# Two buffers for the split second weight of the small slots, and its split and gather moved

## The chip, the cores and the metric

The kernel runs on one core of one Trainium2 chip. It is written by hand for the five engines: PE (TensorE, matmuls), DVE (VectorE), ACT (ScalarE), POOL (GpSimd, which also issues the indirect DMAs: gathers and scatters by a list of rows) and SP (SyncE, which issues plain DMAs). The metric is the device time of one execution in microseconds (us).

## The reference

An attention over channels is followed by a mixture of experts in which each token takes one expert, or none. In short:

```python
qn = q / (norm(q, axis=1) + 1e-06); kn = k / (norm(k, axis=1) + 1e-06)
s = kn.transpose(0, 2, 1) @ qn / tau            # B = 4, N = 5056, C = 256
a = softmax(s)                                  # 256 x 256 for each of the 4
x = (v @ a).reshape(20224, 256)

do_compute = x @ w_skip > 0                     # the other tokens pass through
xc = x[do_compute]
e_idx = argmax(xc @ w_gate)                     # one of E = 8 experts
for e in range(8):
    h = maximum(xc[mask] @ w1[e], 0.0)          # 256 -> 1024
    y[mask] = gate_w[mask] * (h @ w2[e])        # 1024 -> 256
out[do_compute] = xc + y
```

## The kernel before

First come the scores and the attention output of the four batches, written to `out`, and the routing: each expert's tokens are written as a list of rows. The first tiles of the experts run in that stretch too. All of it is set in order by a planner from a table of costs; its tasks are emitted one after the other, and each engine executes its own instructions in the order in which they are emitted. Two loops follow. The **large loop** (L432 in the profile) takes tiles of 512 tokens of one expert, from about 467 to 746 us. The **small loop** (L522) takes what is left of each expert in slots of 128 tokens, ten of them here, two to an iteration, from 750 us to the end.

A product in this kernel is taken with operands that are split into a high part and the remainder: ACT casts the high part, DVE subtracts it from the value (`w1H`, `w1L`; `xH`, `xL`; `v2s` holds both parts of w2). The program's names in the small loop: `v1r`, `v2r` are the slot's w1 and w2 as gathered (two buffers each, 1 MB a buffer), `vc`, `vd` the indices for these gathers, copied by DVE from the table `wii`; `yg` the gathered rows, `yT` their transpose, `yr` a copy for the residual; `yH`, `yL` the split hidden layer; `yo` the slot's output; `mc`, `mN`, `mP`, `ms` the lists of rows of the present slot, of the next ones and for the scatter.

A slot has two stages. In the first, PE multiplies w1 (L539, 32 matmuls into `ph`), ACT takes the relu (L542), DVE the remainder (L543), and w2 is split in four chunks: three ahead of the first half of the hidden layer, one ahead of the second (L501 on ACT, L502 on DVE). POOL gathers w2 for the next slot, copies the list and scatters the output of the slot before (L214). In the second stage PE multiplies w2 (L558 and L559 for each of eight blocks of the hidden layer, into `po`), and after block 4 transposes the next slot's rows (L494; ACT copies `yT` and `yr`, L495 and L496). POOL gathers w1 for the slot after next and rows for it (L209). DVE ends the slot with `yo` (L564, L565).

The loops are staggered: there is no barrier between iterations, but an engine enters a stage only when every engine has signalled the end of the stage two before it. `behind(X)` puts the engine's signal at that place in its order; the instructions after it belong to the stage but aren't waited for. POOL's signal of a first stage stands behind the scatter. A loop is entered through a barrier of all engines; POOL, which collects it, may still be executing work that its sequencer has passed on.

The first rows, lists and weights of the small slots are brought in early: `load_rows` and `load_weights` are tasks of the planner and run at 457 to 468 us, ahead of the large loop (`load_weights`: w1 and w2 of slot 0, w1 of slot 1). On DVE's order the copies of the indices (L511, L512) stand there ahead of the last of the planned tiles (L344, L345) and of the splits for the first tile of the large loop (L311 for w1, L286 for x). A program's tile that is written again waits until the earlier readers are done; for a DMA that reads it, until the DMA has landed. Between the loops stands `keep_warm`, twelve small matmuls (L1129).

Of the kernel before, what the change touches and what calls it, by code (L numbers as in the profile page):

```python
# [12 lines left out]
F32R = mybir.dt.float32r  # L13
I32 = mybir.dt.int32
AF = mybir.ActivationFunctionType
ALU = mybir.AluOpType
# [4 lines left out]
P = 128  # L21
B = 4
N = 5056
C = 256
# [5 lines left out]
NFB = F // P  # L30
# [6 lines left out]
U = 2  # L37
# [106 lines left out]
def attn_moe(ctx: ExitStack, tc: tile.TileContext, q, k, vt, tau, w_skip, w_gate, w1, w2, out):  # L144
    nc = tc.nc
    V, S, G, T = nc.vector, nc.scalar, nc.gpsimd, nc.tensor
# [73 lines left out]
    def gather_w(src, to, rows):  # L220
        G.indirect_dma_start(  # L221
            out=to, out_offset=None, in_=src,
            in_offset=IndirectOffsetOnAxis(ap=rows, axis=0), bounds_check=E * P - 1, oob_is_err=False)
# [8 lines left out]
    def behind(*engines):  # L232

        for e in engines:
            tc.previous_stage_wait(e.engine)
# [3 lines left out]
    class Large:  # L239
# [191 lines left out]
        def loop(self):  # L431
            with tc.For_i(0, self.n, 1, iteration_sync="staggered", hint_engines=(mybir.EngineType.PE,)) as i, tc.manual_schedule():  # L432
                V.tensor_copy(self.wc, self.wii[:, ds(i + 1, 1)])
                V.tensor_copy(self.wd, self.wii[:, ds(i + 1, 1)])
                self.put_last()
                self.take(1)
                self.gather(1)
                gather_w(w1, self.w1r, self.wc)
                behind(G, SP)
                self.first(True)  # L440
                tc.stage_boundary()
                load_list(self.adi, i + 1, self.lN[:, :8, :], 8)
                gather_w(w2, self.w2r, self.wd)
                for t in range(4):
                    self.second(0, t)
                    if t == 1:
                        behind(T, S, V, G, SP)
                        self.transposed(1)
                tc.stage_boundary()
                self.take(0)  # L450
                self.gather(0)
                behind(G, SP)
                self.first(False)
                tc.stage_boundary()
                for t in range(4):
                    if t < 2:
                        self.split_w1(2 * t)
                        self.split_w1(2 * t + 1)
                    self.second(1, t, t < 2)
                    if t == 1:  # L460
                        self.transposed(0)
                        behind(T, S, V, G, SP)
            self.put_last()

    class Small:


        def __init__(self, adi, wii):
            self.adi, self.wii = adi, wii
            wp = ctx.enter_context(tc.tile_pool(name="ws", bufs=1, side="right", reuse_waits="tile"))  # L470
            tiles = lambda shape, dt, name: [wp.tile(shape, dt, name=f"{name}{u}") for u in range(U)]
            self.w1r = tiles([P, 2 * F], F32, "v1r")
            self.w2r = tiles([P, NFB * C], F32, "v2r")
            self.xg = tiles([P, C], F32, "yg")
            self.xr = tiles([P, C], F32, "yr")
            self.xT = tiles([P, 2, P], F32, "yT")
            self.w2s = wp.tile([P, NFB, 2, C], F32R, name="v2s")
            self.hH = wp.tile([P, NFB, P], F32R, name="yH")
            self.hL = wp.tile([P, NFB, P], F32R, name="yL")
            self.ob = tiles([P, C], F32, "yo")  # L480
            self.wc = tiles([P, 1], I32, "vc")
            self.wd = tiles([P, 1], I32, "vd")
            self.lN = tiles([P, 1, 2], I32, "mN")
            self.lP = tiles([P, 1, 2], I32, "mP")
            self.lc = tiles([P, 1, 2], I32, "mc")
            self.ls = tiles([P, 1, 2], I32, "ms")
            for u in range(U):
                V.memset(self.xg[u], 0.0)
                V.memset(self.ob[u], 0.0)
# [8 lines left out]
        def split_w2(self, u, c):  # L498
            f = slice(c * 2, c * 2 + 2)
            r = self.w2r[u][:, c * 512 : (c + 1) * 512].rearrange("p (f c) -> p f c", c=C)  # L500
            S.copy(self.w2s[:, f, 0, :], r)  # L501
            V.tensor_tensor(self.w2s[:, f, 1, :], r, self.w2s[:, f, 0, :], ALU.subtract)  # L502

        def load_rows(self):

# [9 lines left out]
        def load_weights(self):  # L515
            for u in range(U):
                gather_w(w1, self.w1r[u], self.wc[u])
                if u < U - 1:
                    gather_w(w2, self.w2r[u], self.wd[u])

        def loop(self):
            with tc.For_i(0, self.n, U, iteration_sync="staggered") as i, tc.manual_schedule():  # L522
                for u in range(U):
                    o = (u + 1) % U
                    if u:
                        tc.stage_boundary()
                    gather_w(w2, self.w2r[o], self.wd[o])
                    G.tensor_copy(self.ls[o], self.lc[o])  # L528
                    scatter_x(self.ls[o][:, 0, :], self.ob[o])
                    behind(G)  # L530
                    for g in range(2):
                        for c in (0, 1, 2) if g == 0 else (3,):
                            self.split_w2(u, c)
                        ph = psum["h"].tile([P, 512], F32, name="ph")
                        for f in range(4):
                            po = ph[:, f * P : (f + 1) * P]
                            for kb in range(2):
                                fs = slice(kb * F + (4 * g + f) * P, kb * F + (4 * g + f + 1) * P)
                                T.matmul(po, self.w1r[u][:, fs], self.xT[u][:, kb, :], start=(kb == 0), stop=(kb == 1), skip_group_check=True)  # L539
                        fs = slice(4 * g, 4 * g + 4)  # L540
                        hH, hL = (h[:, fs, :].rearrange("p f t -> p (f t)") for h in (self.hH, self.hL))
                        S.activation(hH, ph, AF.Relu)  # L542
                        V.scalar_tensor_tensor(hL, ph, 0.0, hH, ALU.max, ALU.subtract)  # L543
                        if g == 0:
                            behind(T, S, V, SP)
                            V.tensor_copy(self.wc[u], self.wii[:, ds(i + (u + U), 1)])
                            V.tensor_copy(self.wd[u], self.wii[:, ds(i + (u + U), 1)])
                    tc.stage_boundary()
                    G.tensor_copy(self.lc[o], self.lN[o])  # L549
                    G.tensor_copy(self.lN[o], self.lP[o])  # L550
                    load_list(self.adi, i + (u + 2 * U + 1), self.lP[o], 1)
                    behind(SP)
                    gather_w(w1, self.w1r[u], self.wc[u])
                    gather_x(self.xg[u], self.lN[u][:, 0, :])
                    behind(G)
                    po = psum["o", u % 2].tile([P, 512], F32, name="po")
                    for f in range(NFB):
                        T.matmul(po, self.hH[:, f, :], self.w2s[:, f, :, :], start=(f == 0), stop=False, skip_group_check=True)  # L558
                        T.matmul(po[:, :C], self.hL[:, f, :], self.w2s[:, f, 0, :], start=False, stop=(f == NFB - 1), skip_group_check=True)  # L559
                        if f == 4:  # L560
                            self.transposed(o)
                            behind(T, S, V)
                    gate = self.lc[u][:, 0, 1:2].bitcast(F32)
                    V.scalar_tensor_tensor(self.ob[u], po[:, C:], gate, self.xr[u], ALU.mult, ALU.add)  # L564
                    V.scalar_tensor_tensor(self.ob[u], po[:, :C], gate, self.ob[u], ALU.mult, ALU.add)  # L565
            scatter_x(self.lc[U - 1][:, 0, :], self.ob[U - 1])
# [174 lines left out]
    def keep_x(d, jj):  # L741
        S.copy(xos[d][:, jj : jj + 2, :], pxs[d, jj][:, :, :NA])  # L742
# [172 lines left out]
    for c in range(NC):  # L915
# [21 lines left out]
        g = scores(c)  # L937
# [8 lines left out]
        if ch == NCH - 1:  # L946
            g = softmax(b)
            s0, = chain(g, ("S", 0.5), deps=[t])
            n0, = chain(g, ("T", 0.8), deps=[s0, summed[0], summed[1]])
            s = chain(g, ("V", 0.42), ("S", 1.65), ("V", 2.2), ("V", 1.85), ("S", 2.35), ("V", 0.75), deps=[n0])  # L950
# [19 lines left out]
    for d in range(NC):  # L970
# [8 lines left out]
        g = attend(d)  # L979
        t0 = None  # L980
        for j in range(J // 2):
            t = then("B", add("T", 1.475, None, [sv[j > 2][1], sv[j >= 2][1], ready_a[b]], nominal["B", d, j], hold=("px", 2, 1)))
            s = then("xo", add("S", 0.5, lambda d=d, j=j: keep_x(d, 2 * j), [t]))
# [11 lines left out]
        g = route(d)  # L995
        r = chain(g, ("V", 0.43), deps=[lgt] + ([routed[d - 1]] if d else []))
# [10 lines left out]
        if d == NC - 1:  # L1007
            g = end_lists()
# [47 lines left out]
    for x in range(K0):  # L1056
# [4 lines left out]
        for i in range(4):  # L1061
            g = large.first_ahead(2 * i)
# [8 lines left out]
        for i in range(2):  # L1071
            g = large.second_ahead(x, 2 * i)
# [110 lines left out]
```

## Time and profile before

| | |
|---|---|
| three runs | 838.61, 839.3 (median) and 842.23 us |
| the profiled execution | 838.44 us, of which the span is 836.7 |
| large loop's first and last matmul | 466.64 and 745.7 us |
| small loop's first matmul | 750.07 us |
| starts of the ten slots (first product) | 750.07, 757.31, 764.89, 775.50, 782.15, 791.40, 799.54, 808.13, 816.39, 823.31 |
| last output of a slot (`yo`) | 831.59 to 832.07 us |

In the rows of the timeline stand the start, the duration, the engine, the line, the operation with its output and inputs and its shape, and in brackets how long the engine was idle ahead of it and what ended that. Where an engine waits for several things the profile names the one that came last. Times are microseconds from the start of the span.

### The profile page before, as it was taken

Reading aid. Unit: us, or ns where it says so; the run is one execution under the profiler, and the core shown is the slowest. Engines: PE = TensorE matmul, PEld = TensorE weight load, DVE = VectorE, ACT = ScalarE, POOL = GpSimd, SP = SyncE. Lnnn points to the kernel's source line nnn. Section 1 sums busy time; section 2 is a strip of 40 time slices with the busy share of each in tenths; the row PEclk is TensorE's granted clock in tenths of the full one; section 3 lists DMA queues with packets and bytes.
Section 4 is the critical chain, followed back from the end, with each engine's and each line's share of the span. In section 5 each row is a group of like instructions: output and inputs, shape, how many; then the busy total and the mean of one; then the engine's idle time right before and its main releaser. Section 6 shows DMA issues by size and latency. Waiting matters only on the chain. (4 is left out here: it accounts for less than half of the span.)

```text
span 836.7 us, 13561 instructions
## 1 busy us (share of the span) xinstructions
PE 790.2 (94%) x4506; PEld 695.8 (83%) x4506; DVE 519.4 (62%) x1055; ACT 369.8 (44%) x583; POOL 430.5 (51%) x470
## 2 busy tenths in 40 slices
PE   6999999999979999999989699999999999988876
PEld 5888888998968988888878588888888888877876
DVE  4729758989958556455377646465555556455655
ACT  5449548867665425324212424233333333234543
POOL 3000377778657776767427752434343434426666
PEclk9999999999989999999999899999999999999999
DMA  8969869999364535123021521111111111107770
GB/s 322 400 242 361 346 189 297 397 305 340 103 225 135 165 83 191 56 71 114 26 61 53 197 58 38 51 39 56 44 48 46 44 50 44 31 28 254 258 268 4
DMA packets 58073, 126.35 MB, mean 151 GB/s; under 512 B 17556, under 2 KB 37804, under 8 KB 55472
## 3 DMA queue, kind: packets, MB, share of 16 engines
q1 hardware_dynamic: 17280, 62.99, 20.4%
q0 software_dynamic: 19520, 42.12, 15.3%
q10 hardware_dynamic: 21232, 20.72, 8.2%
q8 instruction: 22, 0.36, 0.2%
q14 instruction: 19, 0.16, 0.1%
HBM read 115.98 MB, written 32.59 MB: 178 GB/s over the span
## 5 line engine op out<-in xcount | busy, mean ns | idle before, releaser
L817 POOL DMA_INDIRECT lst<-pay,r_posi x160 | 177.0, 1106 | 164.4 <-DVE r_posi L814 93.1
L662 PE MATMUL s<-qt,kt 128*128 128x256 f32 x640 | 149.2, 384 | 7.7 <-DMA kt<-in_k 7.7
L214 POOL DMA_INDIRECT out<-xg,lc x78 | 81.7, 1047 | 130.0 <-DVE xg L345 112.9
L662 PEld LDWEIGHTS s<-qt,kt 128*128 128x128 f32 x640 | 119.0, 192 | 22.7 <-issue 8.1
L338 PE MATMUL po<-w2s,hH 128*128 128x512 f32 x384 | 136.4, 398 | 1.1 <-ACT hH L321 1.1
L321 ACT ACTIVATE hH<-ph 128x512 fp32r<-128x512 f32 x96 | 57.5, 599 | 127.3 <-PE ph L318 127.3
L339 PE MATMUL po<-w2s,hL 128*128 128x256 f32 x384 | 107.2, 279 | 0.0
L322 DVE SCALAR_TENSOR_TENSOR hL<-ph,hH 128x512 fp32r<-128x512 f32 x96 | 66.5, 692 | 54.1 <-ACT hH L321 52.8
L209 POOL DMA_INDIRECT xg<-out,lc x80 | 83.5, 1044 | 31.6 <-issue 19.5
L735 PE MATMUL px<-aH,vH 128*128 128x266 f32 x320 | 99.1, 310 | 0.3 <-ACT xo L742 0.3
L737 PE MATMUL px<-aH,vL 128*128 128x266 f32 x320 | 91.8, 287 | 0.0
L736 PE MATMUL px<-aL,vH 128*128 128x266 f32 x320 | 91.3, 285 | 0.0
L338 PEld LDWEIGHTS po<-w2s,hH 128*128 128x128 f32 x384 | 72.1, 188 | 18.0 <-ACT hH L321 1.5
L742 ACT COPY xo<-px 128x532 f32<-128x532 f32 x80 | 47.8, 603 | 73.2 <-PE px L737 73.0
L316 PE MATMUL ph<-xH,w1H 128*128 128x512 f32 x192 | 75.7, 394 | 3.4 <-PEq L432 3.4
L338 PE MATMUL px<-w2s,hH 128*128 128x512 f32 x224 | 78.7, 395 | 0.0
L317 PE MATMUL ph<-xL,w1H 128*128 128x512 f32 x192 | 75.4, 393 | 0.0
L318 PE MATMUL ph<-xH,w1L 128*128 128x512 f32 x192 | 75.4, 393 | 0.0
L339 PEld LDWEIGHTS po<-w2s,hL 128*128 128x128 f32 x384 | 72.3, 188 | 0.4
L344 DVE SCALAR_TENSOR_TENSOR xg<-po,lc,xg 128x256 f32<-128x256 f32 x48 | 23.2, 484 | 63.8 <-PE po L339 53.1
L339 PE MATMUL px<-w2s,hL 128*128 128x256 f32 x224 | 62.7, 280 | 0.0
L735 PEld LDWEIGHTS px<-aH,vH 128*128 128x128 f32 x320 | 60.4, 189 | 1.9 <-ACT xo L742 0.5
(205 smaller groups left out, 1591.9 us busy)
## 6 DMA issues: line engine op xcount, KB each, us to landing
vf<-in_vt SPq DMA_DIRECT2D x32, 640.0 KB, 5.3
qt<-in_q SPq DMA_DIRECT2D x31, 640.0 KB, 7.0
kt<-in_k SPq DMA_DIRECT2D x31, 640.0 KB, 7.5
out<-xo ACTq DMA_DIRECT2D x12, 1280.0 KB, 6.4
lst<-pay,r_posi POOLq DMA_INDIRECT x160
out<-xo ACTq DMA_DIRECT2D x4, 640.0 KB, 5.9
out<-xo ACTq DMA_DIRECT2D x4, 576.0 KB, 8.8
xg<-out,lc POOLq DMA_INDIRECT x80, 2.8
```

Of the source, the lines that this page charges most:

```text
L209: apart(G.indirect_dma_start(out=to, out_offset=None, in_=out[0:n, :], in_offset=IndirectOffsetOnAxis(ap=ls[:, 0:1], axis=0), bounds_check ...
L214: i = (G.indirect_dma_start(out=out, out_offset=IndirectOffsetOnAxis(ap=ls[:, 0:1], axis=0), in_=src, in_offset=None, bounds_check=NTOK - ...
L316: T.matmul(ph, self.w1H[:, fs], self.xH[:, kb, :], start=(kb == 0), stop=False)
L317: T.matmul(ph, self.w1H[:, fs], self.xL[:, kb, :], start=False, stop=False)
L318: T.matmul(ph, self.w1L[:, fs], self.xH[:, kb, :], start=False, stop=(kb == 1))
L338: T.matmul(po, self.hH[:, f, ts], self.w2s[:, f, :, :], start=(f == 0), stop=False, skip_group_check=True)
L339: T.matmul(po[:, :C], self.hL[:, f, ts], self.w2s[:, f, 0, :], start=False, stop=(f == NFB - 1), skip_group_check=True)
L662: T.matmul(sums[b][:, cb, :], kt[:, j % JH, cb * P : (cb + 1) * P], qt[:, j % JH, :], start=(ch == 0 and j == 0 and cb == 0), stop=(ch == ...
L735: T.matmul(px[:, i, :NA], vH[:, kb, js], aH[:, kb, :], start=(kb == 0), stop=False)
L736: T.matmul(px[:, i, :NA], vH[:, kb, js], aL[:, kb, :], start=False, stop=False)
L737: T.matmul(px[:, i, :NA], vL[:, kb, js], aH[:, kb, :], start=False, stop=(kb == 1))
L817: i = G.indirect_dma_start(out=lst, out_offset=IndirectOffsetOnAxis(ap=posi[:, t : t + 1], axis=0), in_=pay[:, t0 + t, :], in_offset=None, ...
```

## The change

`v2s` becomes two buffers. The split of w2 for the next slot moves into the second stage: chunks 0 and 1 ahead of the second product, chunks 2 and 3 after block 3, behind the transposes, which stand one block earlier. The gather of w2 in a first stage is for the slot two later and goes to the buffer of the present slot. The index `vd` is copied in the second stage. `load_weights` gathers w2 for both first slots, and then copies the next index into `vd` of slot 0. Slot 0's w2 is split ahead of the loop.

```diff
-            self.w2s = wp.tile([P, NFB, 2, C], F32R, name="v2s")
+            self.w2s = tiles([P, NFB, 2, C], F32R, "v2s")
...
         def load_weights(self):
             for u in range(U):
                 gather_w(w1, self.w1r[u], self.wc[u])
-                if u < U - 1:
-                    gather_w(w2, self.w2r[u], self.wd[u])
+                gather_w(w2, self.w2r[u], self.wd[u])
+            V.tensor_copy(self.wd[0], self.wii[:, U : U + 1])
 
         def loop(self):
+            for c in range(4):
+                self.split_w2(0, c)
             with tc.For_i(0, self.n, U, iteration_sync="staggered") as i, tc.manual_schedule():
...
-                    gather_w(w2, self.w2r[o], self.wd[o])
+                    gather_w(w2, self.w2r[u], self.wd[u])
...
                     for g in range(2):
-                        for c in (0, 1, 2) if g == 0 else (3,):
-                            self.split_w2(u, c)
...
                             V.tensor_copy(self.wc[u], self.wii[:, ds(i + (u + U), 1)])
-                            V.tensor_copy(self.wd[u], self.wii[:, ds(i + (u + U), 1)])
...
                     behind(G)
+                    V.tensor_copy(self.wd[o], self.wii[:, ds(i + (u + 1 + U), 1)])
                     po = psum["o", u % 2].tile([P, 512], F32, name="po")
+                    for c in range(2):
+                        self.split_w2(o, c)
+                    behind(S, V)
                     for f in range(NFB):
...
+                        if f == 3:
+                            self.transposed(o)
+                            for c in range(2, 4):
+                                self.split_w2(o, c)
                         if f == 4:
-                            self.transposed(o)
-                            behind(T, S, V)
+                            behind(T)
```

How this moves instructions is seen at three places. The first is DVE's order ahead of the large loop, after the change, with the semaphores that each row waits for (`px`: output of a planned tile; `pt`: transposed rows; `vd_4868`: index of slot 0's w2).

```order
L345 SCALAR_TENSOR_TENSOR xg_145<-px,lc_153,xg_145 128x256 [waits DVE_49]
L520 COPY vd_4868<-wii_4807 128x1 [waits DMASW2_49]
L311 TENSOR_TENSOR w1L<-w1r,w1H 128x512 [waits DMASW1_49,Activation_49]
L286 TENSOR_TENSOR xL<-pt,xH 128x512 [waits Activation_49]
L311 TENSOR_TENSOR w1L<-w1r,w1H 128x512 [waits Activation_49] x3
L286 TENSOR_TENSOR xL<-pt,xH 128x512 [waits Activation_49]
L432 COMPARE_AND_BRANCH [waits barrier_Pool_Activation_PE_DVE_SP_release]
```

The row of L520 is the only new one there; its semaphore is the one that slot 0's gather of w2 raises when it has landed. All other rows stand as before.

The second is POOL's order at the same place, after the change (`v1r_4850`, `v2r_4852`: w1 and w2 of slot 0; the other two: of slot 1; `out<-xg` stores a planned tile).

```order
L221 DMA w2r<-in_w,wd 128x2048
L221 DMA v1r_4850<-in_w,vc_4866 128x2048
L221 DMA v2r_4852<-in_w,vd_4868 128x2048
L221 DMA v1r_4851<-in_w,vc_4867 128x2048
L221 DMA v2r_4853<-in_w,vd_4869 128x2048
L214 DMA out<-xg_145,lc_153 20224x256 x4
L432 ISA x3
```

The gather into `v2r_4853` is new; it stands ahead of the stores.

The third is DVE's order in the loop's first slot: before,

```order
L502 TENSOR_TENSOR v2s<-v2r_4852,v2s 128x2x256 x3
L543 SCALAR_TENSOR_TENSOR yL<-ph,yH 128x512
L546 ISA
L546 COPY vc_4865<-wii_4807 128x1
L547 ISA
L547 COPY vd_4867<-wii_4807 128x1
L502 TENSOR_TENSOR v2s<-v2r_4852,v2s 128x2x256
L543 SCALAR_TENSOR_TENSOR yL<-ph,yH 128x512
L564 SCALAR_TENSOR_TENSOR yo_4863<-po,mc_4873,yr_4856 128x256
L565 SCALAR_TENSOR_TENSOR yo_4863<-po,mc_4873,yo_4863 128x256
```

and after the change (the ISA rows read the loop's counter or wait for a stage):

```order
L544 SCALAR_TENSOR_TENSOR yL<-ph,yH 128x512
L547 ISA
L547 COPY vc_4866<-wii_4807 128x1
L544 SCALAR_TENSOR_TENSOR yL<-ph,yH 128x512
L556 ISA
L556 COPY vd_4869<-wii_4807 128x1
L503 TENSOR_TENSOR v2s_4861<-v2r_4853,v2s_4861 128x2x256 x4
L571 SCALAR_TENSOR_TENSOR yo_4864<-po,mc_4874,yr_4856 128x256
L572 SCALAR_TENSOR_TENSOR yo_4864<-po,mc_4874,yo_4864 128x256
```

The four subtractions, now of the next slot's w2, stand behind both halves of `yL` and ahead of `yo`. On ACT the four casts move in the same way, and four casts and four subtractions for slot 0 stand ahead of the loop.

More of the change, by code (lines that the diff above doesn't have):

```diff
@@ L500, in split_w2 @@
             r = self.w2r[u][:, c * 512 : (c + 1) * 512].rearrange("p (f c) -> p f c", c=C)
-            S.copy(self.w2s[:, f, 0, :], r)
-            V.tensor_tensor(self.w2s[:, f, 1, :], r, self.w2s[:, f, 0, :], ALU.subtract)
+            s = self.w2s[u][:, f, :, :]
+            S.copy(s[:, :, 0, :], r)
+            V.tensor_tensor(s[:, :, 1, :], r, s[:, :, 0, :], ALU.subtract)
         def load_rows(self):
@@ L555, in loop @@
                     behind(G)
+                    V.tensor_copy(self.wd[o], self.wii[:, ds(i + (u + 1 + U), 1)])
                     po = psum["o", u % 2].tile([P, 512], F32, name="po")
+                    for c in range(2):
+                        self.split_w2(o, c)
+                    behind(S, V)
                     for f in range(NFB):
-                        T.matmul(po, self.hH[:, f, :], self.w2s[:, f, :, :], start=(f == 0), stop=False, skip_group_check=True)
-                        T.matmul(po[:, :C], self.hL[:, f, :], self.w2s[:, f, 0, :], start=False, stop=(f == NFB - 1), skip_group_check=True)
+                        T.matmul(po, self.hH[:, f, :], self.w2s[u][:, f, :, :], start=(f == 0), stop=False, skip_group_check=True)
+                        T.matmul(po[:, :C], self.hL[:, f, :], self.w2s[u][:, f, 0, :], start=False, stop=(f == NFB - 1), skip_group_check=True)
+                        if f == 3:
+                            self.transposed(o)
+                            for c in range(2, 4):
+                                self.split_w2(o, c)
                         if f == 4:
-                            self.transposed(o)
-                            behind(T, S, V)
+                            behind(T)
                     gate = self.lc[u][:, 0, 1:2].bitcast(F32)
```

## The prediction

> **What bounds the kernel now.** I read the busy table first, then the slices of the stretch that the change touches, then its timelines. TensorE (PE) is busy for most of the span, so an edit counts only where it moves PE or the ends of the stages.
>
> ```profile
> span 836.7 us, 13561 instructions
> PE 790.2 (94%) x4506; PEld 695.8 (83%) x4506; DVE 519.4 (62%) x1055; ACT 369.8 (44%) x583; POOL 430.5 (51%) x470
> ```
>
> The diff touches two stretches. The ten small slots run from 750 us to the end. The preparation that `Small` orders ahead of the large loop stands at 457 to 477 us. For the first, the view of waits from 752 to 832 us (waiting instruction, releaser, total us, times, longest) gives the stake:
>
> ```profile
> POOL out L214 <- DMA yg<-out,mN: 7.8, 4, 2.3
> PE po L558 <- DVE v2s L502: 5.4, 5, 1.8
> PE po L558 <- DVE yL L543: 4.5, 2, 2.3
> ```
>
> The second product (`po`) waits 9.9 us in all, and the trace names the split of w2 (`v2s`) for 5.4 of them. The change moves just this split. Whether it is the true releaser is read from the timelines (start, duration, engine, work, idle time ahead and its releaser). First the slot at 764.9 us, then one after it, then the loop's first:
>
> ```profile
> 764.89 3.81 PE L539 MATMUL ph<-yT,v1r 128*128 128x128 f32 x32
> 769.09 0.67 DVE L502 TENSOR_TENSOR v2s<-v2r,v2s 128x512 fp32r<-128x512 f32 x1
> 770.18 1.02 POOL L214 DMA_INDIRECT out<-yo,ms  x1 [2.30 <-DMA yg<-out,mN]
> 770.90 0.77 PE L558 MATMUL po<-v2s,yH 128*128 128x512 f32 x1 [2.20 <-DVE yL L543]
> ...
> 775.50 3.73 PE L539 MATMUL ph<-yT,v1r 128*128 128x128 f32 x32
> 782.15 3.80 PE L539 MATMUL ph<-yT,v1r 128*128 128x128 f32 x32
> 787.57 1.02 POOL L214 DMA_INDIRECT out<-yo,ms  x1 [2.34 <-DMA yg<-out,mN]
> 788.28 0.47 PE L558 MATMUL po<-v2s,yH 128*128 128x512 f32 x1 [2.33 <-DVE yL L543]
> ```
>
> At 769.09 + 0.67 = 769.76 the split is over, yet `po` starts at 770.90, 0.72 after POOL's scatter. In the slot of 782.15 it starts 0.71 after the scatter, which itself waited 2.34 us for a gather of rows to land. PE enters a stage only when POOL has signalled the stage two before, and POOL's signal stands behind this scatter. So the landing of a gather holds `po`, not the split. In the first slot `po` even runs ahead of the last split:
>
> ```profile
> 753.55 0.68 DVE L502 TENSOR_TENSOR v2s<-v2r,v2s 128x512 fp32r<-128x512 f32 x1
> 753.64 0.48 PE L558 MATMUL po<-v2s,yH 128*128 128x512 f32 x1
> ```
>
> So the named releaser is only the last one seen. I put the gain in the slots at **0**, with 9.9 us as the other end.
>
> **The preparation: the block on VectorE (DVE).** The new copy of an index, `V.tensor_copy(self.wd[0], ...)` in `load_weights`, overwrites the very index that slot 0's gather of w2 reads. So it waits until this gather has landed. In DVE's order it stands between the last L345 and the first L311 of these rows:
>
> ```profile
> 460.62 0.48 DVE L345 SCALAR_TENSOR_TENSOR xg<-px,lc,xg 128x256 f32<-128x256 f32 x1
> 461.02 0.68 DVE L311 TENSOR_TENSOR w1L<-w1r,w1H 128x512 fp32r<-128x512 f32 x1
> ...
> 464.02 0.68 DVE L286 TENSOR_TENSOR xL<-pt,xH 128x512 fp32r<-128x512 f32 x1
> 466.32 0.15 DVE L433 COPY wc<-wii 128x1 int32 x1 [1.61 <-PEq L432]
> ```
>
> Behind it are queued the four splits of w1 and the two of x for the large loop's first tile; PE waits for these, and the loop's entry waits for DVE. PE and POOL there:
>
> ```profile
> 462.36 0.66 PE L282 MATMUL pt<-ident,xg 128*128 128x128 f32 x4 [1.65 <-DVE xL L286]
> 466.64 0.76 PE L316 MATMUL ph<-xH,w1H 128*128 128x512 f32 x1 [3.41 <-PEq L432]
> ...
> 462.87 1.50 POOL L221 DMA_INDIRECT v1r<-in_w,vc  x1 [0.30 <-issue]
> 464.68 0.99 POOL L221 DMA_INDIRECT v2r<-in_w,vd  x1 [0.30 <-issue]
> 477.23 0.19 POOL L265 COPY lc<-lN 128x8 int32<-128x8 int32 x1 [1.68 <-DMA out<-xg,lc]
> ```
>
> When does slot 0's w2 land? The table of windows (busy time by engine, granted clock, DMA share, GB/s):
>
> ```profile
> 465.00:468.25 3.25, 1.60 (x4) 1.34 (x5) 0.29 (x2) 0.00 (x0) 2.64 (x3) 0.50 0.91 325
> 468.25:470.75 2.50, 2.50 (x8) 1.94 (x7) 0.49 (x1) 1.11 (x2) 1.89 (x3) 0.57 1.00 416
> 470.75:476.60 5.85, 5.85 (x27) 4.86 (x26) 5.14 (x9) 3.92 (x7) 3.88 (x4) 1.00 0.89 315
> 476.60:480.00 3.40, 2.94 (x13) 2.09 (x12) 1.61 (x3) 1.62 (x3) 1.86 (x3) 1.00 0.07 14
> ```
>
> A tile of 128x2048 float32 is 1.049 MB. 3.25 us at 325 GB/s are 1.056 MB: slot 0's w1, issued first. 2.5 us at 416 are 1.040 MB: slot 0's w2. The next 1.84 MB are slot 1's w1 and six stores of 0.13 MB, so the sum closes. W2 is thus moved by 470.75; the stores' traffic ends at 476.60 and POOL goes on at 477.23, so a landing is seen about 0.6 later: **471.35**. The Trainium skill, DMA: Bandwidth & Descriptors, section "Anatomy of one DMA — SWDGE (gpsimd) path", fits a lone transfer at 2.0 us plus its bytes over 436 GB/s, an estimate of 4.4 us here, so w2 would land at 469.1 and the sum be 2.2 less. The rows speak against that: until 468.25 the engines are taken with w1's bytes.
>
> From the block's end DVE needs what it needs now, 461.02 to 464.70, 3.68 us; then 1.94 to PE's first matmul (464.70 to 466.64). 471.35 + 0.1 + 3.68 + 1.94 = 477.07 instead of 466.64: **+10.4**. Something is given back. Now PE stops in the first tile:
>
> ```profile
> 480.68 0.47 PE L338 MATMUL po<-w2s,hH 128*128 128x512 f32 x1 [1.15 <-ACT hH L321]
> ```
>
> POOL could not signal there until its stores had landed (477.23). With the loop 10 us later and the stores only 2.5 us later, this wait goes: −1.15. The slow clock of the first matmuls (0.50 and 0.57 in the windows) comes after a pause of 3.41 us; after a longer one it is paid once too. Net **A = +9.2**, between 8.2 (nothing for the visible landing; 1.5 us of entry) and 10.9 (landing 0.5 later, the 1.15 not given back).
>
> One more gather of w2, 1.05 MB, joins the queue: 1.049/0.416 = 2.5 us of DMA and about 1.0 of POOL, both over at 479.1 to 479.8, 2 to 3 us into the delayed loop. They hide behind the block; without it they would show.
>
> **The entry to the small loop.** Four casts and four subtractions for slot 0 now come ahead of the loop's barrier instead of beside its first product.
>
> ```profile
> 746.26 0.48 DVE L345 SCALAR_TENSOR_TENSOR xg<-po,lc,xg 128x256 f32<-128x256 f32 x1
> 746.95 1.58 PE L1129 MATMUL m<-ones 128*128 128x128 f32 x12 [1.25 <-PEq L432]
> 749.67 1.66 ACT L501 CAST v2s<-v2r 128x512 fp32r<-128x512 f32 x3 [8.84 <-SPq L522]
> 750.07 3.81 PE L539 MATMUL ph<-yT,v1r 128*128 128x128 f32 x32 [1.54 <-issue]
> 750.51 1.94 DVE L502 TENSOR_TENSOR v2s<-v2r,v2s 128x512 fp32r<-128x512 f32 x3 [3.77 <-ACT v2s L501]
> ```
>
> Both engines are free at about 746.9. Here the third subtraction ends 752.45 − 749.67 = 2.8 us after the first cast starts; with a fourth (0.6) DVE is done at 746.9 + 3.4 = 750.3 at most, and 749.3 if cast and subtraction overlap as closely as 0.55 apart. PE's warm-up ends at 748.53. So the barrier opens 0.8 to 1.8 later; part of that wait is paid today at POOL's stores, so **B = +0.9**, between 0.3 and 1.8. PE then idles 2.4 us instead of 1.54.
>
> **Inside the slots.** w2's gather now waits on the split, and the scatter on `yo`, which two subtractions push 1.0 us back. The scatter stands 7.8 us in four slots for the landing, 2.3 at most, which covers that in the slots that set the pace, so **C = 0**. In a slot without such a wait the 1.0 could show once before the next landing hides it: C lies between −9.9 and +1.0. The gathers of w2 are as many as before, and one slot earlier, so they land with time to spare. The transposes, one step earlier in PE's order, cost the same.
>
> **The end.** In the last slot the casts of chunks 2 and 3 and their subtractions, for a slot that doesn't exist, stand ahead of `yo`:
>
> ```profile
> 830.29 0.41 ACT L496 COPY yr<-yg 128x256 f32<-128x256 f32 x1
> 831.59 0.48 DVE L565 SCALAR_TENSOR_TENSOR yo<-po,mc,yo 128x256 f32<-128x256 f32 x1
> 833.10 1.02 POOL L214 DMA_INDIRECT out<-yo,mc  x1 [0.91 <-PEq L1179]
> ```
>
> `yr` ends at 830.70, or 830.35 with the transposes a step earlier; two casts of 0.55 and the last subtraction of 0.68 give 832.1 before `yo`, which began at 831.07: **D = +0.7** at the last scatter, between 0.2 and 1.0.
>
> **Sum.** 9.2 + 0.9 + 0 + 0.7 = +10.8 on the profiled execution's 838.44 us (836.7 of it the span): 849.2. The median of the three runs is 0.9 above that execution, so I take **849.5**. About 0.5% (4.2 us) is what a measurement of this kernel tells from no change.
>
> **Rivals.** *The split did hold the second product.* Place: L558 in seven slots. Then the slots go at PE's own pace, 782.15 − 775.50 = 6.65 us, and ten of them take 66.5 where 750.07 to 831.03 is 81.0: at most −14.5, at least the named −9.9. With A, B and D paid that is 834.7 to 839.3, on the faster side if the loop through the landing gets shorter too. Against it stand the scatter rows. It decides if `po` in the slots of 764.9 and 782.15 follows the scatter by less than now. Chance 0.08, half of it faster. *The copy doesn't hold DVE*, because the landing is earlier or the copy stands elsewhere. Then only the extra gather remains: the stores land 2.5 later, PE's stop at 480.68 becomes 483.2, and 838.44 + 2.5 + 0.9 + 0.7 = 842.5, up to 844.2 with a slow clock. Chance 0.08. *A slow clock more.* After the idle 2.20 us at 770.90 the matmuls take 0.63 instead of 0.40, seven of them, about 1.6 us; after 2.33 at 788.28 they don't. PE's pause at the small loop's entry grows to this size, and the phase in other slots shifts: 851 to 853.5. Chance 0.12. The Trainium skill, TensorE: Matmul & The Clock Gate, section "Part 1: The HAM clock gate", lets the clock fall only after an idle window of about 3.4 us. By that this rival would fall away and the forecast stand; the row at 770.90 disagrees.
>
> The forecast has 0.72. The range is 843.5 to 853.5: the bounds of A to D as far as they can fall together, the slow clock and the upper half of the second rival. Faster 0.04, same 0.07, slower 0.89.
>
> **What would show it.** Right: in the new trace an index copy on DVE at about 471.4 with an idle stretch of 10 us ahead of it, the large loop's first matmul at about 477, no stop of PE some 14 us after it, then all of the loop 9 us later; `po` in the slots still 0.7 after the scatter; last `yo` 1 us further behind its product. Wrong: DVE's L311 still at 461, or slots of 6.7 us each.

## The result and the profile after

The changed kernel takes 850.77 us in the median of four runs (848.32 to 852.38), the kernel before 838.95: a ratio of 1.013 with a 95% interval of 1.0092 to 1.0168. It is slower, by 11.8 us.

The timeline of the changed kernel ahead of the large loop, first DVE, then PE (start, duration, engine, work, idle time ahead and what ended it):

```profile
461.81 0.48 DVE L345 SCALAR_TENSOR_TENSOR xg<-px,lc,xg 128x256 f32<-128x256 f32 x1
472.10 0.15 DVE L520 COPY vd<-wii 128x1 int32<-128x1 int32 x1 [9.81 <-DMA v2r<-in_w,vd]
472.18 0.69 DVE L311 TENSOR_TENSOR w1L<-w1r,w1H 128x512 fp32r<-128x512 f32 x1
...
473.53 1.11 PE L282 MATMUL pt<-ident,xg 128*128 128x128 f32 x4 [11.62 <-DVE xL L286]
476.83 0.77 PE L316 MATMUL ph<-xH,w1H 128*128 128x512 f32 x1 [1.76 <-DVE xL L286]
```

The copy of one index, 0.15 us long, keeps DVE waiting 9.81 us for the landing of slot 0's w2. The splits of w1 stand right behind it, and PE waits 11.62 us for DVE's first x (`xL`). The large loop starts at 476.83 instead of 466.64.

The windows of the changed kernel over the same stretch (busy time by engine, granted clock, DMA share, GB/s):

```profile
466.00:469.00 3.00, 0.00 (x0) 0.00 (x0) 0.00 (x0) 0.00 (x0) 2.23 (x3) 0.50 0.83 336
469.00:472.00 3.00, 0.00 (x0) 0.00 (x0) 0.00 (x0) 0.00 (x0) 2.25 (x3) 0.50 1.03 429
472.00:475.00 3.00, 1.47 (x6) 1.14 (x6) 2.90 (x6) 0.32 (x1) 1.72 (x2) 0.50 1.02 404
475.00:478.00 3.00, 1.24 (x4) 1.01 (x4) 1.25 (x4) 0.84 (x3) 0.00 (x0) 0.50 0.94 313
478.00:482.00 4.00, 4.00 (x11) 3.13 (x10) 1.29 (x2) 1.10 (x2) 2.10 (x3) 0.50 0.32 116
482.00:486.00 4.00, 4.00 (x18) 3.24 (x17) 2.86 (x5) 3.13 (x6) 2.78 (x4) 0.98 0.15 42
```

For six microseconds PE, DVE and ACT do nothing at all while the share of the DMA engines is 0.83 and 1.03. The slow clock also lasts longer into the tile, from the first matmul at 476.83 to 482, 5.2 us where it was 3.7 (466.64 to 470.3).

The small loop's entry, ACT, DVE and PE:

```profile
756.67 2.18 ACT L502 CAST v2s<-v2r 128x512 fp32r<-128x512 f32 x4 [6.11 <-PEq L432]
757.32 2.49 DVE L503 TENSOR_TENSOR v2s<-v2r,v2s 128x512 fp32r<-128x512 f32 x4 [0.84 <-ACT v2s L502]
756.69 1.58 PE L1136 MATMUL m<-ones 128*128 128x128 f32 x12 [1.25 <-PEq L432]
760.42 3.81 PE L540 MATMUL ph<-yT,v1r 128*128 128x128 f32 x32 [2.15 <-PEq L525]
```

DVE's last subtraction ends at 759.81, PE's warm-up at 758.27: the barrier opens for DVE, and PE idles 2.15 us where it idled 1.54. In the slots, a scatter and the product behind it, and three lines of the view of waits from 762 to 842 us:

```profile
796.56 1.02 POOL L214 DMA_INDIRECT out<-yo,ms  x1 [1.64 <-DMA yg<-out,mN]
797.16 0.47 PE L562 MATMUL po<-v2s,yH 128*128 128x512 f32 x1 [1.82 <-issue]
...
POOL out L214 <- DMA yg<-out,mN: 5.1, 3, 1.9
PE po L562 <- ACT yH L543: 5.0, 4, 1.3
PE po L562 <- issue: 4.8, 4, 2.0
```

In the three slots whose scatter waits for a landing, the second product still starts 0.60 us behind the scatter. In the slots between them (the fourth, sixth and eighth) it waits 1.21 to 1.28 us too, and starts 1.33 to 1.42 us behind a scatter that waits for no landing; what releases it there the profile doesn't show. The split is no longer named as the releaser, since it was done before; the wait is there all the same, 9.8 us against 9.9, under other names. At the end:

```profile
839.20 1.14 ACT L502 CAST v2s<-v2r 128x512 fp32r<-128x512 f32 x2
839.72 0.28 PE L563 MATMUL po<-v2s,yL 128*128 128x256 f32 x1
839.85 1.29 DVE L503 TENSOR_TENSOR v2s<-v2r,v2s 128x512 fp32r<-128x512 f32 x2 [0.95 <-ACT v2s L502]
841.06 0.48 DVE L571 SCALAR_TENSOR_TENSOR yo<-po,mc,yr 128x256 f32<-128x256 f32 x1
843.08 1.01 POOL L214 DMA_INDIRECT out<-yo,mc  x1 [1.66 <-PEq L1186]
```

PE is done at 840.00, and `yo` waits 1.1 us more for two subtractions of a slot that doesn't exist.

The span is cut at five starts for all that follows: the first index copy of `load_rows` on DVE (458.07 before, 459.47 after), the large loop's first matmul, the warm-up, the first and the tenth slot's first matmul, and the last `yo` (L565 before). Each entry is the difference of two such starts, in us.

| kernel (profiled execution) | index copy to large loop | large loop to warm-up | warm-up to slots | first to tenth slot | tenth slot to last `yo` |
|---|---|---|---|---|---|
| before | 8.57 | 280.31 | 3.12 | 73.24 | 8.28 |
| before, again | 8.48 | 280.29 | 2.92 | 72.03 | 7.37 |
| after | 17.36 | 279.86 | 3.73 | 72.06 | 9.10 |
| after, again | 19.02 | 279.18 | 3.72 | 74.00 | 9.14 |
| e1, copy late (slower chip) | 8.79 | 282.45 | 3.72 | 74.02 | 9.12 |
| e9, copy late | 9.06 | 284.08 | 3.73 | 72.27 | 9.10 |
| e7, and `yo` first | 9.09 | 284.99 | 3.73 | 73.87 | 8.39 |
| e5, copy and gather late (slower chip) | 8.63 | 283.31 | 3.73 | 75.51 | 9.34 |
| e2, before with the copy (slower chip) | 17.86 | 279.81 | 2.92 | 71.54 | 8.22 |
| e3, before with the gather (slower chip) | 9.00 | 283.16 | 2.93 | 71.85 | 7.58 |
| e4, no split in the slots | 8.36 | 281.71 | 3.87 | 71.02 | 7.44 |
| e6, no w1 gather in the slots | 8.42 | 280.19 | 3.09 | 66.10 | 7.36 |
| e8, before with w1 first | 8.43 | 281.61 | 3.12 | 70.56 | 7.78 |
| e10, all of it | 9.13 | 284.02 | 3.73 | 73.53 | 7.54 |

### The profile page after: what moved, and what is told of

It is laid out like the page before. It is cut to its first block, busy times and chain, and to the rows that moved or that the text cites. A ratio compares the mean times of both kernels' runs of the same rounds, so it can differ in the third digit from the quotient of the medians.

```text
span 846.7 us, 13573 instructions
## 1 busy us (share of the span) xinstructions
PE 791.0 (93%) x4506; PEld 696.8 (82%) x4506; DVE 523.2 (62%) x1060; ACT 371.7 (44%) x587; POOL 430.2 (51%) x471
## 5 line engine op out<-in xcount | busy, mean ns | idle before, releaser
L284 ACT CAST xH<-pt 128x512 fp32r<-128x512 f32 x40 | 22.4, 591 | 92.0 <-PE pt L282 85.5
```

## The experiments

**The copy alone.** Four runs (e1, e2, e3 and e5) stood on a chip on which every kernel was slower (896.54 us for the kernel before), nearly all of it ahead of the index copies, which come at 512 to 516 us there instead of 458 to 462. The kernel before was not traced there. Of the one edit that was traced on both kinds of chip (e1 and e9) the stretches agree within 0.3 us but for the large loop and the slots, so the comparison goes by the stretches.

```diff
# e1 and e9, against the changed kernel
         def load_weights(self):
...
-            V.tensor_copy(self.wd[0], self.wii[:, U : U + 1])
 
         def loop(self):
+            V.tensor_copy(self.wd[0], self.wii[:, U : U + 1])
             for c in range(4):
                 self.split_w2(0, c)
# e2, against the kernel before
                 if u < U - 1:
                     gather_w(w2, self.w2r[u], self.wd[u])
+            V.tensor_copy(self.wd[0], self.wii[:, U : U + 1])
```

> The changed kernel with one line moved: the new index copy into vd of slot 0 stands behind the large loop, ahead of slot 0's splits, not among the preparations. Theory (the copy's wait for slot 0's w2 blocks VectorE ahead of the large loop): the pause of VectorE there goes, the large loop starts at 466.5 to 468 us, and of the changed kernel's +10 some 8 to 10 go; what remains is the extra gather (0 to 2.5), the entry (0.6) and the end (0.8): 839 to 843 us. Rival (the extra 1 MB of gather, or the split in its new places, costs the time; the copy's wait is incidental): 848 to 851 us.

> The kernel before with only the index copy into vd of slot 0 added behind the gathers of load_weights. Theory: VectorE waits 9 to 10 us for the landing of slot 0's w2, the large loop starts at 476 to 477 us, total 847.5 to 849.5. Rival (copy incidental): 838 to 840 us.

On the slower chip e1 measured 899.49 us, a ratio of 1.0034 (0.9992 to 1.0076), e2 900.72, 1.0093 (1.0053 to 1.0132). The changed kernel and e1 once more, on chips of the usual speed:

> The changed kernel unchanged, on the same chip as its experiments. Theory: 17.4 us from the index copies to the large loop's first matmul, 279.8 from there to the warm-up, 3.7 from the warm-up to the slots, 81 to 83 in the slots. Against the kernel before on this chip +6 to +10.

> e1_copy_late once more, in the hope of a chip with the usual speed, since its first run stood on one where every kernel took some 7% longer. Theory (the wait of the copy is the cost): 8.4 to 8.8 us from the index copies to the large loop's first matmul; from there to the warm-up 280.3 plus up to 2.5 for the extra gather; 3.7 to the slots; 81 to 83 in the slots: 840 to 843, that is +1 to +4 against before. Rival (the wait is incidental): 848 to 851.

The changed kernel came to 850.96 us, 1.0139 (1.0112 to 1.0165). That is 11.9 more than the kernel before on its chip, above the 6 to 10 that I expected; the stretch with the block took 19.02 us in its trace, not 17.4. With the copy moved it is 844.4, 1.0075 (1.0049 to 1.0102). The timeline of e2, DVE and PE:

```profile
525.89 0.15 DVE L520 COPY vd<-wii 128x1 int32<-128x1 int32 x1 [8.63 <-DMA v2r<-in_w,vd]
...
530.65 0.77 PE L316 MATMUL ph<-xH,w1H 128*128 128x512 f32 x1 [1.79 <-DVE xL L286]
```

One line put into the kernel before makes the stretch 17.86 us long (DVE waits 8.63 us, a little less than the 9 to 10 expected), where the eleven traces without it there have 8.4 to 9.1; moved out of there in the changed kernel, it gives the stretch its old length back. The block is shown in both directions. But e9 lies above the 840 to 843 that I expected, and the move brings only 6.6 us by the medians, 5.4 by the ratios, not 8 to 10: the large loop takes 284.08 instead of 279.2 to 279.9.

**The extra gather.**

```diff
# e3, against the kernel before
-                if u < U - 1:
-                    gather_w(w2, self.w2r[u], self.wd[u])
+                gather_w(w2, self.w2r[u], self.wd[u])
# e5, against e1
-                gather_w(w2, self.w2r[u], self.wd[u])
+                if u < U - 1:
+                    gather_w(w2, self.w2r[u], self.wd[u])
...
+        gather_w(w2, smalls[0].w2r[1], smalls[0].wd[1])
         keep_warm(6)
         smalls[0].loop()
```

> The kernel before with only the gather of slot 1's w2 added to load_weights (the loop's own gather of it stays, so slot 1's w2 is brought twice). Theory: the large loop starts as before; the stores ahead of it land up to 2.5 us later, and PE's stop in the first tile (480.68 us, 1.15 us) grows by 1 to 2.5: 840 to 842.5 us. Rival (the extra gather is the cost): 846 us or more. If the stop has room: 839.

> e1_copy_late, and slot 1's w2 is gathered behind the large loop as well, ahead of the warm-up matmuls. Theory: the first tile's stop of PE is as in the kernel before (about 1.1 us), so 1 to 2.5 us less than e1_copy_late; POOL reaches its first scatter in the small loop about 1.3 us later, which can give 1.3 back: 838.5 to 841. If the extra gather was free in e1_copy_late: no less than that run.

E3 measured 896.74 us, 1.0039 (0.9989 to 1.0088), e5 902.35, 1.0109 (1.0036 to 1.0182). By times e3 tells nothing. E5 is a miss: its five stretches sum to 380.5 us, e1's to 378.1, and its first slot alone takes 10.58 us against 8.28. The first product is not the cause, since it takes 5.44 us, at the slow clock, in both. But the second one stands idle for 1.46 us ahead of its start in e5 and not at all in e1, and ACT's casts ahead of it wait for w2 to land: the late gather runs into the small loop. Nor do these two settle the gather, since e5's large loop, without it there, is as long as e3's on that chip.

On the other chips it is seen. Three traces have the gather and no block (e9, e7, e10), and their large loops take 284.02 to 284.99 us; the five that have neither (before twice, e4, e6, e8) take 280.19 to 281.71. That puts it at 2.3 to 4.8 us. No run takes the gather alone out of e9 there, so this is a comparison of traces and not a test; and the stop of PE in the first tile varies without it too: it lasts 0.81 to 1.15 us in three of the five, but 2.29 in e4 and 2.44 in e8, and why wasn't followed up. E9 in detail: POOL's take after the stores, PE's stop, and two windows:

```profile
480.12 0.19 POOL L265 COPY lc<-lN 128x8 int32<-128x8 int32 x1 [2.75 <-DMA out<-xg,lc]
...
483.58 0.47 PE L338 MATMUL po<-w2s,hH 128*128 128x512 f32 x1 [3.57 <-issue]
...
479.50:484.00 4.50, 0.93 (x5) 0.49 (x4) 1.20 (x2) 0.60 (x1) 2.65 (x4) 1.00 0.10 29
484.00:488.00 4.00, 4.00 (x16) 3.42 (x15) 0.00 (x0) 0.00 (x0) 3.08 (x4) 0.57 0.41 105
```

POOL goes on after the stores 12.75 us after the loop's start (467.37) instead of 10.59, PE stops 3.57 us instead of 1.15, and after the stop the clock is 0.57 for four microseconds more. The stop is 2.4 longer than in the first trace of the kernel before. Behind it, the 32nd of the matmuls `po<-w2s,hH` starts 13.32 us after the first instead of 11.71, which is 1.6 for the clock, and ahead of it 0.3 is won, so the large loop is 3.8 us longer (284.08 − 280.31). In the changed kernel the loop starts ten microseconds later and none of this is seen. The block of DVE hid it.

**What holds the second product.**

> The kernel before unchanged, for a trace on the chip of the experiments. Both theories: from the index copies of load_rows to the large loop's first matmul 8.6 us (8.56 in the first trace); no gather of w2 in VectorE's way. From that matmul to the warm-up 280.3 if PE's stop in the first tile is 1.15 as in the first trace, up to 283 if it is 2 to 4 as in the runs without the block. Ten slots: 79.5 to 80 from the first matmul to the last yo without a slow clock in a slot, 81.5 with.

```diff
# e4, against the kernel before (slot 0's w2 serves every slot)
+            for c in range(4):
+                self.split_w2(0, c)
             with tc.For_i(0, self.n, U, iteration_sync="staggered") as i, tc.manual_schedule():
...
-                        for c in (0, 1, 2) if g == 0 else (3,):
-                            self.split_w2(u, c)
# e6, against the kernel before (the first two slots' w1 serves every slot)
-                    gather_w(w1, self.w1r[u], self.wc[u])
```

> The kernel before with the splits of w2 taken out of the slots (slot 0's w2 is split once, ahead of the loop, and used for all). Theory (the landing of a gather holds the second product, not the split): the ten slots take what they take in the kernel before, 79.5 to 81.5 us from the first matmul to the last yo, and the second product still starts 0.6 to 0.7 after the scatter in the slots where the scatter waits for a landing. Rival (the split holds it): the slots get shorter by 5.4 to 9.9 us, 70 to 76.

> The kernel before without the gathers of w1 in the slots (the first two slots' w1 is used for all). Theory: the gathered rows land up to 2.5 us sooner in the slots with a real w1 gather, the scatter and the second product with them, and the slots run nearer to PE's 6.65 us: 68 to 75 us from the first matmul to the last yo. Rival (the split holds the second product): 79 to 81.5, as before.

The kernel before measured 837.44 us once more, 0.9986 (0.9968 to 1.0005); e4 838.03, 0.999 (0.9971 to 1.0009); e6 833.08, 0.9914 (0.9885 to 0.9942). In e4 the splits are gone altogether, and against the kernel before, taken again, neither the total nor the ten slots (71.02 against 72.03) move by more than some 1 us. To the last `yo` that is 78.5 us, 1.0 less than I expected at least, and not the 70 to 76 of the rival. A scatter and the product behind it in e4, and two lines of its waits from 752 to 832 us:

```profile
790.12 1.02 POOL L214 DMA_INDIRECT out<-yo,ms  x1 [2.67 <-DMA yg<-out,mN]
...
790.72 0.47 PE L558 MATMUL po<-v2s,yH 128*128 128x512 f32 x1 [1.64 <-ACT yH L542]
...
POOL out L214 <- DMA yg<-out,mN: 8.3, 4, 2.7
PE po L558 <- ACT yH L542: 7.8, 6, 1.6
```

With no split to name, the profile names another input that came late, `yH`, for 7.8 us of wait; some 1 to 2 of the 9.9 may have been the split's. In e6's view of waits from 752 to 832 us no scatter waits for a landing; what is left is

```profile
POOL out L214 <- POOL ms L528: 5.5, 10, 0.8
```

a copy of the list on POOL itself. The waits of 1.0 to 1.3 us in the slots between are in e4 still and in e6 under 0.2, and the slots shrink by 5.9 us to 66.10, with times between 68 and 75 to the last `yo` as expected (66.10 + 7.36 = 73.46). So w1's gather in front of the rows holds the slots. Whether by its bytes or by the time that POOL takes to issue it, e6 doesn't tell, since both are gone there.

**Better versions.**

```diff
# e7, against e9
                         if f == 3:
                             self.transposed(o)
-                            for c in range(2, 4):
-                                self.split_w2(o, c)
...
                     V.scalar_tensor_tensor(self.ob[u], po[:, :C], gate, self.ob[u], ALU.mult, ALU.add)
+                    for c in range(2, 4):
+                        self.split_w2(o, c)
# e8, against the kernel before; e10: the same against e7
                     tc.stage_boundary()
+                    gather_w(w1, self.w1r[u], self.wc[u])
                     G.tensor_copy(self.lc[o], self.lN[o])
...
-                    gather_w(w1, self.w1r[u], self.wc[u])
                     gather_x(self.xg[u], self.lN[u][:, 0, :])
```

> e9_copy_late_again with the split of chunks 2 and 3 put behind yo. Theory: from the last slot's first matmul to its last yo 7.4 to 8.3 us as in the kernel before, not 9.1, so 0.8 to 1.7 us less than e9_copy_late_again; the other slots unchanged, or 0.3 less where the scatter waits for yo. If the end isn't held by these splits: no difference.

> The kernel before with one line moved: in a slot's second part POOL gathers w1 ahead of the two copies of lists, not behind them. Theory (the landing of w1 and of the rows behind it sets the pace of the slots): w1 is issued some 0.9 us sooner in each slot, so the slots that wait for a landing take up to 0.9 less, 66 to 70 us from the first slot to the tenth where the kernel before took 72.0, total 833 to 838. If the landing doesn't set the pace: 72 as before.

> e7_copy_late_yo_first with w1 gathered ahead of the list copies too. Theory: the slots as in e8_before_w1_first, so 2 to 6 us less than e7_copy_late_yo_first. If what the change kept (the split a slot ahead) is worth something once the landing is sooner: less than e8_before_w1_first in the slots; if not: the same there, and 1 to 3 more in all for the extra gather and the entry.

E7 measured 847.46 us, 1.0091 (1.0058 to 1.0124). Its last slot gets 0.7 shorter, just short of the 0.8 to 1.7 expected, but the ten slots 1.6 longer, and the total is no better than e9's; what lengthened the slots wasn't followed up. E8 measured 838.04, 0.9981 (0.9962 to 0.9999): the slots take 70.56 instead of 72.03, short of the 66 to 70 expected, and the total ends just below the kernel before, by 0.7 us in the medians. A gain that small isn't told from chance by one trace, since the same slots took 71.5 to 72.0 in e2, e3 and the second trace of before. E10 measured 843.44, 1.0055 (1.0036 to 1.0073): better than e7 by 4 us, as expected, not than the kernel before. Its trace is of its slowest execution (846.8), with a first slot of 9.42 us at the slow clock, so its slots (73.53) say little. No version with the early split came below the kernel before.

## Why the prediction was right

I predicted 849.5 us, slower; it measured 850.77. By its own terms, in the spans of the two pairs of traces (836.7 to 846.7, and, taken again, 834.6 to 849.0):

| term | predicted | first pair | taken again |
|---|---|---|---|
| A: index copy to warm-up | +9.2 | 8.79 − 0.45 = +8.3 | 10.54 − 1.11 = +9.4 |
| B: warm-up to slots | +0.9 | +0.6 | +0.8 |
| C: first to tenth slot | 0 | −1.2 | +2.0 |
| D: last slot to last `yo` | +0.7 | +0.8 | +1.8 |
| ahead of the index copy, and the tail | 0 | +1.4 | +0.4 |
| sum | +10.8 | +10.0 | +14.4 |

- **The block** is the mechanism foretold; its size is right in part by luck. The copy stood at 472.10 where 471.35 was worked out, and the loop started at 476.83 where 477.07 was, but the whole stretch began 1.4 us later in this trace than in that of before, for no reason that a run shows. The stretch itself grew by 8.79 us in the first pair and by 10.54 in the second, where +10.4 was worked out; the copy waited 9.81 and 11.34 us for its landing.
- **What is given back** in the first tile was put at 1.15 us, PE's stop. In the first pair it is 0.45: the stop did go, but I had the slow clock paid alike in both, and it lasted 1.5 us longer. The 25th matmul of the loop starts 8.05 us after the first instead of 7.29, which is 0.76 lost. In the second pair the slow clock lasted as long in both (7.45 and 7.43), and 1.11 is given back.
- **The entry** takes 3.72 or 3.73 us in all seven traces with the early split, and 2.92 to 3.12 in the six that split in the slots: +0.6 to +0.8 where +0.9 was put.
- **The slots.** The split is not what sets their pace (e4), w1's gather and the landing behind it are (e6), and the change gives nothing there. The reading that the scatter holds the second product fits the three slots whose scatter waits for a landing; for the three between, the releaser stays open. The −1.2 of the first pair comes from a slot at the slow clock in the first trace of before (10.61 us; with the two slots behind it 1.6 us longer than in the second). The +2.0 of the second pair comes from the first slots of the changed kernel. There the third rival's slow clock came at the loop's entry: the first product took 5.44 us (the row below), where after the same 2.15 us of idle time it took 3.81 in the first trace, and the first three slots are 1.8 us longer. A slot of 10.29 us later in that trace costs only 0.1, since the next one is shorter by 1.3. So that rival's mechanism came in one of the two traces, though neither median (850.77 and 850.96) reaches its 851 to 853.5.
- **The extra gather**, costed at nothing behind the block, is not seen there. Without the block I had it at 2.5 us and 842.5 in all, with a slow clock 844.2 as the upper end; e9 measured 844.4, with 2.4 for the stop and 1.6 for the clock.
- **The end** depends on how late the last slot stands before (7.37 and 8.28 in two traces, 9.10 and 9.14 after), so D is 0.8 to 1.8, not 0.7.
- The sums of the two pairs, +10.0 and +14.4, stand on either side of the 11.8 by the medians. That 10.8 lies so near it is in part chance, since single terms are off by up to 2 us.

The first product of the small loop in the second trace of after:

```profile
760.72 5.44 PE L540 MATMUL ph<-yT,v1r 128*128 128x128 f32 x32 [2.15 <-PEq L525]
```

## What to carry to other kernels

An index that a gather reads must not be overwritten right behind the gather by an engine with other work in its queue: 0.15 us of copying held VectorE until the landing, 8.6 to 11.3 us, and everything queued behind it. The releaser that a profile names for a wait on several things is the last one, not always the one that pays to move. A start at a fixed distance from something else, here the scatter, is a hint; the test is to take the named work away, as e4 does. And a cost hidden behind a new wait is not gone: take the wait away, and price it again.

## What the runs showed of the hardware

The clock of PE fell after pauses much shorter than the one ahead of the large loop. In the second trace of after, the product of the seventh slot and the windows around it:

```profile
816.12 0.53 PE L562 MATMUL po<-v2s,yH 128*128 128x512 f32 x1 [1.91 <-issue]
...
814.00:816.00 2.00, 0.21 (x2) 0.02 (x1) 0.91 (x3) 0.68 (x2) 0.48 (x1) 1.00 0.85 254
816.00:818.00 2.00, 1.88 (x7) 1.67 (x8) 1.45 (x3) 1.06 (x2) 1.53 (x4) 0.60 0.68 283
818.00:820.00 2.00, 2.00 (x9) 1.76 (x9) 0.00 (x0) 0.76 (x3) 1.69 (x2) 0.55 0.15 42
```

After a pause of 1.91 us the clock was 0.60 and 0.55 for four microseconds; after 2.33 us at 788.28 in the kernel before it stayed up. Nor does the same pause always do the same: after 2.15 us at the entry of the small loop the first product took 5.44 us in four traces (after taken again, e1, e5, e10) and 3.81 in three (after, e7, e9). The Trainium skill, TensorE: Matmul & The Clock Gate, section "Part 1: The HAM clock gate", gives an idle window of about 3.4 us for this; here 1.91 and 2.20 us have been enough. And one chip of those used took 896.54 us for the kernel that others run in 839, with the index copies some 54 us late; the cause of that was not looked for.
